# Pacing a background weight preparation by its own transfers, and a finer seam between two phases

## Chip, core and metric

One Trainium2 chip, one core of it, one launch. The metric is the time of an execution on the device in microseconds (us), as the median of several runs. Beside it stands one profiled execution, from which all rows below come; its span runs from the first instruction of the program to the last.

## What is computed

An attention over 4 batches and 8 heads of 64 (512 local tokens with a window of 32 to each side, 32 global tokens that see and are seen by all) and behind it two layers of a feed-forward kind, 512 to 2048 to 512, each without a residual. Weights of the second layer are `moe2`. Inputs are 32-bit floats but the weights arrive as 64-bit ones.

```
    a_l = sm(s_l)                        # local queries: 32 global keys and the window
    out_l = np.matmul(a_l, np.concatenate([v_g, v_l], axis=2))
    out_g = np.matmul(sm(s_g), v_all)    # global queries: all keys
...
    h = x @ w_in                         # first layer
    relu6 = np.clip(h + 3.0, 0.0, 6.0)
    g = h * relu6 / 6.0
    return (g @ w_out).astype(np.float32)
...
    h = x @ w_in                         # second layer
    alpha = 1.0
    g = np.where(h > 0.0, h, alpha * (np.exp(np.minimum(h, 0.0)) - 1.0))
    return (g @ w_out).astype(np.float32)
```

## The kernel before

The 2176 tokens are 17 tiles of 128 (16 local ones and `G`, the global tokens of all batches), put together to five chunks of 4, 3, 3, 3 and 4 tiles. Products keep about the accuracy of 32-bit floats by cutting each operand into a rounded part and a rest (`high`, `low`, names ending in h and l) and adding three matmuls (`mm3`, L541, where nearly all matmuls are recorded).

**Order of work.** The start is an order written out by hand (`SCHED`). From then on the program is a list of steps (layer, chunk, f), f being one of 16 blocks of 128 of the inner 2048. A step has `up` (12 matmuls into the tile h), `act` (on ScalarE g at L567 and the cast gh at L573, on VectorE the product at L568 and the rest gl), and `down` of the step two before it (`LAG`), which adds to the tiles acc. A step has three places (part 0, 1, 2), with the two halves of `down` between them. At these places stands other work: while chunk c runs, the attention of chunk c+1 in stages (scores S on TensorE at L349, minimum on VectorE, exponentials P on ScalarE at L362; transposes T at L90 and their copies PT; values O; then x), and at the end of a place the weight preparation. At the last block of a chunk the tiles acc are copied to `ev` (L603 on ScalarE, L605 on VectorE, three buffers) and stored to `x2d` (L607). Each engine, and SP, which issues all DMAs, works off its own instructions in the order in which the program writes them.

**The second layer.** Chunk 1 (`STD2`) is computed like the first layer, in 16 steps after the last of layer one. The chunks (2, 3) and (0, 4) are computed in pairs by class `Super`, with seven products (`up(g, k)` into ua and ub) in place of eight for each of 8 pairs of blocks and each pair of chunks. Product k of ua may be added to the tile ua only when ScalarE has copied what stands in it (tiles s, L790, L797, L800). `go` issues the next product or the next group of output matmuls (`down_a` into acc, `down_b` into yt) and then what `after(n, ...)` has put off by n turns.

**The preparation.** `prepare` is a generator that makes the second layer's weights ready while layer one runs, in eight pairs p of blocks: for each of four raw pieces of 512 KB a load (`load`, L163, tile raw), `first` (ScalarE, L167: scales the upper word into wi or wo), `second` and `third` (VectorE, L170 to L176: put the bits together), `high` (ScalarE cast, L182: tiles ha, hb, oa, ob), `low` (VectorE, L186) and `out` (L189: store of 512 KB to `wd`); in between the sums `sf` of the pieces for the seven products, cast and stored as sa and sb. Six stores for each pair. Later `load_stream` (L726) loads wd back as the tiles ws. Four buffers f0 to f3 take all of it, in the roles A, B_, W and X; what writes a buffer has to wait for the store or the readers of what it held.

The generator yields (gap, VectorE cost, ScalarE cost) ahead of each piece. `Pace.step` is called once at each place, three times a step; it lets a piece go when the last piece lies `gap` places back and when the work that it has counted for the two engines leaves room:

```
                gap, dve, act = self.cost
                if self.gap < gap or (dve and self.dve + dve > ROOM) or (act and self.act + act > ROOM):
                    return
```

Of the kernel before, what the change touches and what calls it, by code (L numbers as in the profile page):

```python
# [26 lines left out]
NF = DFF // P  # L27
# [32 lines left out]
ROOM = 2.25  # L60
# [8 lines left out]
def tile_kernel(ctx, tc, qkW, vW, qkG, vN, vG, masks, w1, w2, out):  # L69
# [83 lines left out]
    def prepare():  # L153
# [3 lines left out]
        def roles(p):  # L157
            return ("f0", "f2", "f1", "f3") if p % 2 == 0 else ("f2", "f0", "f3", "f1")

# [32 lines left out]
        nxt = load(0, 0, 0, "f0"), load(0, 1, 0, "f2")  # L192
        for p in range(NF // 2):
            A, B_, W, X = roles(p)
            ra, rb = nxt
            yield 1 if p else 3, 0, 1.2
# [3 lines left out]
            first(wb, rb)  # L200
            yield 1, 0.7, 0
            second(w)
            yield 0, 1.4, 0
            third(wa, ra)
            yield 0, 1.4, 0.6
            ha = high(shaped(wa, 2), 2, f"ha{p}", X)
            third(wb, rb)
            yield 0, 0.7, 0.6
            oa = load(p, 0, 1, B_)
            hb = high(shaped(wb, 2), 2, f"hb{p}", A)  # L210
            low(ha, shaped(wa, 2))
            yield 1, 0.7, 0
            low(hb, shaped(wb, 2))
            yield 1, 0, 0
            out(ha, p, 0)
            yield 1, 0, 0
            out(hb, p, 2)
            yield 2, 0.8, 0
# [3 lines left out]
            nc.vector.tensor_sub(sf[:, 0], sf[:, 2], half(wa, 0))  # L222
            yield 0, 0.8, 0
            nc.vector.tensor_sub(sf[:, 1], half(wa, 0), half(wb, 0))
            nc.vector.tensor_sub(sf[:, 3], half(wa, 1), sf[:, 0])
            yield 0, 0, 0.6
            s1 = high(sf[:, :2], 2, f"sa{p}", W)
            yield 1, 0.7, 0.6
            s2 = high(sf[:, 2:], 2, f"sb{p}", A)
            low(s1, sf[:, :2])  # L230
            yield 1, 0.7, 0
            low(s2, sf[:, 2:])
            yield 1, 0, 0
            out(s1, p, 8)
            yield 1, 0, 0.6
            out(s2, p, 10)
            w = pool.tile([P, 2, DM], I32, name=f"wo{p}", tag=X, bufs=1)
            wa, wb = w[:, 0], w[:, 1]
            first(wa, oa)
            yield 0, 0.4, 0  # L240
            second(wa)
            ob = load(p, 1, 1, W)
            yield 0, 1.4, 0
            third(wa, oa)
            yield 1, 0, 1.2
            ha = high(shaped(wa, 1), 1, f"oa{p}", A)
            first(wb, ob)
            yield 1, 1.1, 0
            low(ha, shaped(wa, 1))
            second(wb)  # L250
            yield 0, 1.4, 0
            if p + 1 < NF // 2:
                nxt = (load(p + 1, 0, 0, B_),)
            third(wb, ob)
            yield 1, 0, 0.6
            out(ha, p, 4)
            hb = high(shaped(wb, 1), 1, f"ob{p}", W)
            yield 1, 0.7, 0
            low(hb, shaped(wb, 1))
            if p + 1 < NF // 2:  # L260
                nxt += (load(p + 1, 1, 0, A),)
            yield 1, 0, 0
            out(hb, p, 6)

    class Pace:
# [788 lines left out]
```

## Time and profile before

| | |
|---|---|
| median of 3 runs | 880.34 us (878.87 to 880.65) |
| the profiled execution | 884.33 us, its span 882.3 us |
| TensorE (PE) busy | 851.4 us, 97% of the span |
| VectorE (DVE), ScalarE (ACT) busy | 516.7 us (59%), 429.1 us (49%) |
| granted clock of TensorE, mean | 0.992 |
| moved by DMA | 178.42 MB, 202 GB/s |

A busy share is a mean over stages: the start (to 85 us), layer one with the attention of the next chunk (to about 420), its last chunk without attention (to 513), the plain chunk of the second layer (to 585) and the paired chunks (to the end). Idle time stands in brackets behind an instruction in the timelines, with the instruction that ended it.

### The profile page before, as it was taken

What the parts mean: (1) busy time and instruction counts of PE and PEld (TensorE: products, weight loads), DVE (VectorE), ACT (ScalarE), POOL (GpSimd) and SP (SyncE); (2) the same over time, 40 slices, a digit from 0 to 9 for tenths busy, and PEclk for the clock granted to TensorE, in tenths of its full rate; (3) what the DMA queues carried; (4) which work ended last, traced back from release to release, by engine and by line L of the source; (5) the groups of instructions that cost most, each with busy time, mean ns of one, the idle gap of its engine ahead of it and who ended that gap; (6) DMA issues with size and microseconds to landing.
All of it is one profiled execution on the core that took longest, in us unless ns stands there. A gap on an engine that the chain in (4) does not pass through costs nothing.

```text
span 882.3 us, 15805 instructions
## 1 busy us (share of the span) xinstructions
PE 851.4 (97%) x6424; PEld 731.6 (83%) x6424; DVE 516.7 (59%) x1123; ACT 429.1 (49%) x835; POOL 4.8 (1%) x8
## 2 busy tenths in 40 slices
PE   8899999999799997999899999999999999999998
PEld 7667878898699886989788889988899888888886
DVE  5888974565547655666565544435456674444453
ACT  6576654454444434554443334545454664444442
POOL 0000000000000000000010000000000000000000
PEclk9999999999999999999999999999999999999999
DMA  9947223566645666663678973558662738444102
GB/s 370 418 190 318 81 96 107 176 198 221 220 166 199 225 226 200 216 218 106 217 258 294 352 272 157 204 188 312 238 247 88 286 133 321 143 143 143 48 1 95
DMA packets 37656, 178.42 MB, mean 202 GB/s; under 512 B 4304, under 2 KB 6224, under 8 KB 25680
## 3 DMA queue, kind: packets, MB, share of 16 engines
q1 hardware_dynamic: 37584, 177.42, 55.6%
q8 instruction: 50, 0.82, 0.4%
q14 instruction: 22, 0.18, 0.1%
HBM read 143.33 MB, written 34.08 MB: 201 GB/s over the span
## 4 chain that ended last, share of the span: by engine, by line
PE 75%; DVE 9%; DMA 9%; ACT 5%; issue 2%; SPq 0%; ACTq 0%; DVEq 0%
PE acc L541 26%; PE h L541 19%; PE yt L541 9%; PE ua L541 9%; PE ub L541 6%; DMA wd<-sa 2%; DMA raw<-in_w 2%; DMA wd<-ha 2%; PE T L90 2%; DMA v<-in_vW 1%; DVE g L568 1%; PE O L381 1%; DVE f L134 1%; PE S L349 1%; ACT g L567 1%
## 5 line engine op out<-in xcount | busy, mean ns | idle before, releaser
L541 PE MATMUL acc<-gh,w 128*128 128x384 f32 (+1 forms) x640 | 199.5, 366 | 3.4 <-DVE ev L605 1.7
L541 PE MATMUL h<-x1h,w 128*128 128x384 f32 (+1 forms) x640 | 198.1, 371 | 1.6 <-DVE w L148 1.5
L541 PEld LDWEIGHTS h<-x1h,w 128*128 128x128 f32 x640 | 120.6, 192 | 20.4 <-issue 5.5
L541 PEld LDWEIGHTS acc<-gh,w 128*128 128x128 f32 x640 | 118.7, 188 | 17.9 <-DVE ev L605 2.5
L541 PE MATMUL h<-x1l,w 128*128 128x384 f32 (+1 forms) x320 | 116.7, 365 | 0.2 <-DVE x1l L413 0.2
L541 PE MATMUL acc<-gl,w 128*128 128x384 f32 (+1 forms) x320 | 115.3, 360 | 0.8 <-DVE gl L575 0.8
L573 ACT CAST gh<-g 128x384 fp32r<-128x384 f32 (+1 forms) x96 | 52.8, 550 | 81.5 <-DVE g L568 71.5
L541 PE MATMUL ua<-xs,ws 128*128 128x384 f32 (+1 forms) x384 | 88.0, 364 | 2.1 <-ACT s L790 1.5
L568 DVE SCALAR_TENSOR_TENSOR g<-g,h 128x384 f32<-128x384 f32 (+1 forms) x80 | 48.4, 605 | 65.0 <-ACT g L567 64.6
L541 PEld LDWEIGHTS ua<-xs,ws 128*128 128x128 f32 x384 | 70.3, 188 | 12.9 <-ACT s L790 1.8
L575 DVE TENSOR_TENSOR gl<-g,gh 128x384 fp32r<-128x384 f32 (+1 forms) x96 | 57.4, 598 | 25.9 <-ACT gh L573 25.3
L567 ACT ACTIVATE g<-h,half 128x384 f32<-128x384 f32 (+1 forms) x80 | 49.7, 621 | 39.8 <-PE h L541 39.6
L541 PEld LDWEIGHTS h<-x1l,w 128*128 128x128 f32 x320 | 61.4, 192 | 6.1 <-DVE x1l L413 0.5
L541 PE MATMUL ub<-xs,ws 128*128 128x384 f32 (+1 forms) x288 | 65.7, 363 | 0.0
L541 PEld LDWEIGHTS acc<-gl,w 128*128 128x128 f32 x320 | 60.2, 188 | 6.4 <-DVE gl L575 1.2
L541 PEld LDWEIGHTS ub<-xs,ws 128*128 128x128 f32 x288 | 52.7, 188 | 7.1
L842 DVE TENSOR_TENSOR y<-yt,y 128x512 f32<-128x512 f32 x49 | 33.8, 690 | 34.6 <-PE yt L541 34.1
L757 ACT ACTIVATE e<-c 128x384 f32<-128x384 f32 (+1 forms) x48 | 27.8, 579 | 51.3 <-DVE c L793 19.6
L541 PE MATMUL yt<-ws,gg_h 128*128 128x512 f32 x160 | 49.9, 393 | 0.0
L541 PE MATMUL acc<-ws,gg_h 128*128 128x512 f32 x160 | 49.9, 393 | 0.0
L760 DVE SCALAR_TENSOR_TENSOR e<-e,c 128x384 f32<-128x384 f32 (+1 forms) x48 | 30.0, 624 | 26.0 <-ACT e L758 25.4
L758 ACT ACTIVATE e<-e 128x384 f32<-128x384 f32 (+1 forms) x64 | 37.1, 579 | 2.0
(201 smaller groups left out, 1269.2 us busy)
## 6 DMA issues: line engine op xcount, KB each, us to landing
ws<-wd SPq DMA_DIRECT2D x48, 1024.0 KB, 5.3
raw<-in_w SPq DMA_DIRECT2D x16, 1024.0 KB, 11.6
raw<-in_w SPq DMA_DIRECT2D x32, 512.0 KB, 4.6
v<-in_vW SPq DMA_DIRECT2D x13, 1040.0 KB, 7.1
qk<-in_qkW SPq DMA_DIRECT2D x15, 704.0 KB, 6.1
qkG<-in_qkG SPq DMA_DIRECT2D x8, 608.0 KB, 5.1
wd<-ha SPq DMA_DIRECT2D x8, 512.0 KB, 7.9
wd<-hb SPq DMA_DIRECT2D x8, 512.0 KB, 8.4
```

The source lines that it names most:

```text
L90: nc.tensor.transpose(o, i, ident)
L134: nc.vector.scalar_tensor_tensor(w, self.high[:, s], -0x80000000, w, op0=ALU.bitwise_and, op1=ALU.bitwise_or)
L349: nc.tensor.matmul(self.sp[r][cs, j, :], self.q[rs, j, cs], self.k[rs, j, 32 * i : 32 * i + P], start=True, stop=True,)
L541: nc.tensor.matmul(o, a, b, start=first and i == 0, stop=last and i == len(pairs) - 1, skip_group_check=more)
L567: nc.scalar.activation(g, hp, AF.Relu, scale=1.0 / 6.0, bias=half)
L568: nc.vector.scalar_tensor_tensor(g, g, 1.0, hp, op0=ALU.min, op1=ALU.mult)
L573: nc.scalar.copy(gh, g)
L575: return lambda: nc.vector.tensor_sub(gl, g, gh.bitcast(F32))
L757: nc.scalar.activation(e, h, AF.Relu, scale=-1.0)
L758: nc.scalar.activation(e, e, AF.Exp, scale=-1.0)
L760: 1, lambda: nc.vector.scalar_tensor_tensor(e, e, -1.0, h, op0=ALU.add, op1=ALU.max)
L842: nc.vector.tensor_add(y, o, y)
```

## The change

`FETCH` and `STORE` are two new constants, 3 each. `Pace` counts places in `now` from its start, and a piece names the place from which it may go: three places behind the load whose data it reads (`tw`, `ta`, `tb` hold that place), three behind the store of the buffer that it overwrites, one behind the cast whose rest it takes, two behind the computation whose result it stores. The roles of the four buffers are dealt out otherwise: ha and hb are cast into the buffers of their own raw pieces (A and B_), the sums stand in X, sa and sb follow ha and hb, and all raw pieces of `w_out` go through W. `first` and `second` of two pieces are apart. `step` also runs in the second layer while pieces are left, with costs for what stands there, and a pair of blocks is loaded back only when `done` says that its stores are issued. At the end of the plain chunk `go` is called behind every group of three output matmuls in place of every half of `down`, and the activation of c21 is put off by two turns in place of one.

```diff
-ROOM = 2.25
+ROOM, FETCH, STORE = 2.25, 3, 3
...
-        def roles(p):
-            return ("f0", "f2", "f1", "f3") if p % 2 == 0 else ("f2", "f0", "f3", "f1")
...
-        nxt = load(0, 0, 0, "f0"), load(0, 1, 0, "f2")
+        A, B_, W, X = "f0", "f2", "f1", "f3"
+        ra, rb = load(0, 0, 0, A), load(0, 1, 0, B_)
+        ta = tb = pace.now
         for p in range(NF // 2):
-            A, B_, W, X = roles(p)
-            ra, rb = nxt
-            yield 1 if p else 3, 0, 1.2
+            yield ta + FETCH, 0, 0.6
             w = pool.tile([P, 2, DM], I32, name=f"wi{p}", tag=W, bufs=1)
             wa, wb = w[:, 0], w[:, 1]
             first(wa, ra)
-            first(wb, rb)
-            yield 1, 0.7, 0
-            second(w)
+            yield pace.now + 1, 0.4, 0
+            second(wa)
             yield 0, 1.4, 0
             third(wa, ra)
-            yield 0, 1.4, 0.6
-            ha = high(shaped(wa, 2), 2, f"ha{p}", X)
+            yield tb + FETCH, 0, 0.6
+            first(wb, rb)
+            yield pace.now + 1, 0.4, 0.6
+            ha = high(shaped(wa, 2), 2, f"ha{p}", A)
+            second(wb)
+            yield 0, 1.4, 0
             third(wb, rb)
             yield 0, 0.7, 0.6
-            oa = load(p, 0, 1, B_)
-            hb = high(shaped(wb, 2), 2, f"hb{p}", A)
             low(ha, shaped(wa, 2))
-            yield 1, 0.7, 0
+            la = pace.now
+            hb = high(shaped(wb, 2), 2, f"hb{p}", B_)
+            yield pace.now + 1, 0.7, 0
             low(hb, shaped(wb, 2))
-            yield 1, 0, 0
-            out(ha, p, 0)
-            yield 1, 0, 0
-            out(hb, p, 2)
-            yield 2, 0.8, 0
+            lb = pace.now
+            yield 0, 0.8, 0
             sf = pool.tile([P, 4, 2 * P], F32, name=f"sf{p}", tag=X, bufs=1)
             half = lambda v, k: v.bitcast(F32)[:, 2 * P * k : 2 * P * k + 2 * P]
             nc.vector.tensor_add(sf[:, 2], half(wb, 0), half(wb, 1))
             nc.vector.tensor_sub(sf[:, 0], sf[:, 2], half(wa, 0))
+            yield la + 2, 0, 0
+            out(ha, p, 0)
+            ta = pace.now
             yield 0, 0.8, 0
             nc.vector.tensor_sub(sf[:, 1], half(wa, 0), half(wb, 0))
             nc.vector.tensor_sub(sf[:, 3], half(wa, 1), sf[:, 0])
-            yield 0, 0, 0.6
-            s1 = high(sf[:, :2], 2, f"sa{p}", W)
-            yield 1, 0.7, 0.6
-            s2 = high(sf[:, 2:], 2, f"sb{p}", A)
+            tw = pace.now
+            yield lb + 2, 0, 0
+            out(hb, p, 2)
+            tb = pace.now
+            yield tw + 2, 0, 0
+            oa = load(p, 0, 1, W)
+            tw = pace.now
+            yield ta + STORE, 0, 0.6
+            s1 = high(sf[:, :2], 2, f"sa{p}", A)
+            yield pace.now + 1, 0.7, 0
             low(s1, sf[:, :2])
-            yield 1, 0.7, 0
+            la = pace.now
+            yield tb + STORE, 0, 0.6
+            s2 = high(sf[:, 2:], 2, f"sb{p}", B_)
+            yield pace.now + 1, 0.7, 0
             low(s2, sf[:, 2:])
-            yield 1, 0, 0
+            lb = pace.now
+            yield la + 2, 0, 0
             out(s1, p, 8)
-            yield 1, 0, 0.6
-            out(s2, p, 10)
+            ta = pace.now
+            yield tw + FETCH, 0, 0.6
             w = pool.tile([P, 2, DM], I32, name=f"wo{p}", tag=X, bufs=1)
             wa, wb = w[:, 0], w[:, 1]
             first(wa, oa)
+            yield lb + 2, 0, 0
+            out(s2, p, 10)
+            tb = pace.now
             yield 0, 0.4, 0
             second(wa)
-            ob = load(p, 1, 1, W)
             yield 0, 1.4, 0
             third(wa, oa)
-            yield 1, 0, 1.2
+            yield pace.now + 2, 0, 0
+            ob = load(p, 1, 1, W)
+            tw = pace.now
+            yield ta + STORE, 0, 0.6
             ha = high(shaped(wa, 1), 1, f"oa{p}", A)
+            yield pace.now + 1, 0.7, 0
+            low(ha, shaped(wa, 1))
+            la = pace.now
+            yield tw + FETCH, 0, 0.6
             first(wb, ob)
-            yield 1, 1.1, 0
-            low(ha, shaped(wa, 1))
+            yield pace.now + 1, 0.4, 0
             second(wb)
+            yield la + 2, 0, 0
+            out(ha, p, 4)
+            ta = pace.now
             yield 0, 1.4, 0
+            third(wb, ob)
+            tw = pace.now
+            yield tb + STORE, 0, 0.6
+            hb = high(shaped(wb, 1), 1, f"ob{p}", B_)
+            yield pace.now + 1, 0.7, 0
+            low(hb, shaped(wb, 1))
+            lb = pace.now
+            yield tw + 2, 0, 0
             if p + 1 < NF // 2:
-                nxt = (load(p + 1, 0, 0, B_),)
-            third(wb, ob)
-            yield 1, 0, 0.6
-            out(ha, p, 4)
-            hb = high(shaped(wb, 1), 1, f"ob{p}", W)
-            yield 1, 0.7, 0
-            low(hb, shaped(wb, 1))
+                ra = load(p + 1, 0, 0, W)
+            tw = pace.now
+            yield lb + 2, 0, 0
+            out(hb, p, 6)
+            pace.done = p + 1
+            yield ta + STORE, 0, 0
             if p + 1 < NF // 2:
-                nxt += (load(p + 1, 1, 0, A),)
-            yield 1, 0, 0
-            out(hb, p, 6)
+                rb = load(p + 1, 1, 0, A)
+            ta, tb = tw, pace.now
+            A, B_, W, X = W, A, X, B_
 
...
-        def __init__(self, work, n):
-            self.work, self.left, self.gap = work, n, 0
-            self.cost = next(work)
+        def __init__(self):
+            self.now = self.done = 0
             self.dve = self.act = 0.0
+            self.cost = 0, 0, 0
+
+        def start(self, work):
+            self.work, self.cost = work, next(work)
         def step(self, long, dve, act):
+            self.now += 1
             self.dve = max(0.0, self.dve - long) + dve
             self.act = max(0.0, self.act - long) + act
-            self.gap += 1
             while self.cost is not None:
-                gap, dve, act = self.cost
-                if self.gap < gap or (dve and self.dve + dve > ROOM) or (act and self.act + act > ROOM):
+                earliest, dve, act = self.cost
+                if self.now < earliest or (dve and self.dve + dve > ROOM) or (act and self.act + act > ROOM):
                     return
                 self.dve, self.act = self.dve + dve, self.act + act
-                self.gap = 0
                 self.cost = next(self.work, None)
+
+    pace = Pace()
...
-    def down(m, c, f, part):
+    def down(m, c, f, part, then=None):
...
             mm3(acc[i], pairs, f == 0, f == NF - 1)
             if f == NF - 1:
                 drain(m, c, i)
+            if then is not None:
+                then()
...
                 nc.vector.tensor_add(c21, self.b, self.s2)
-                self.after(1, lambda: self.act(g, 2, c21))
+                self.after(2, lambda: self.act(g, 2, c21))
...
-        pace = Pace(prepare(), NF)
+        pace.start(prepare())
+        back = 0
...
-                if m == 0:
+                if m == 1:
+                    loads = [(1.2 * (part == 1 and 3 <= f < 12), 1.1 * (part == 1 and 5 <= f < 12)) for part in range(3)]
+                if pace.cost is not None:
...
                 if part == 0 and cur is not None:
                     late()
                 if part < 2:
-                    down(*old, part)
-                    if cur is None:
-                        sup.go()
-            if old[:2] == (0, last) and old[2] % 2:
-                sup.load_stream(-1 - old[2] // 2)
+                    down(*old, part, sup.go if cur is None else None)
+            while back < NF // 2 and old >= (0, last, 2 * back + 1) and pace.done > back:
```

What this does to the order is shown at three places. First ScalarE where chunk 2 of layer one begins (g_2_0 is its first activation, P the exponentials of its first attention tile, wo, oa and raw_1_... belong to pair 1). Before:

```order
L573 CAST gh_1_15_2764<-g_1_15_2763 128x384
L167 ACTIVATE wo_2770<-raw_1_0_1_2568 128x512
L182 CAST oa_2784<-wo_2770 128x512
L167 ACTIVATE wo_2770<-raw_1_1_1_2773 128x512
L567 ACTIVATE g_2_0_2808<-h_2_0_2795,half 128x384
L573 CAST gh_2_0_2809<-g_2_0_2808 128x384
L362 ACTIVATE P_2814<-P_2814,mn_2818 128x128 x8
```

Of the change:

```order
L605 CAST gh_1_15_2765<-g_1_15_2764 128x384
L164 ACTIVATE wo_2771<-raw_1_0_1_2703 128x512
L599 ACTIVATE g_2_0_2803<-h_2_0_2790,half 128x384
L605 CAST gh_2_0_2804<-g_2_0_2803 128x384
L394 ACTIVATE P_2809<-P_2809,mn_2813 128x128 x8
L179 CAST oa_2873<-wo_2771 128x512
```

The cast oa and the `first` of the second output piece (raw_1_1_1) stood ahead of g_2_0, gh_2_0 and P; now oa stands behind P, and that `first` is no longer among these rows.

Second, SP and ScalarE where chunk 3 begins, with pair 3. SP before (v and qk are loads of the attention, the stores to wd and raw of the preparation):

```order
L320 DMA qk_3795<-in_qkW 128x1408
L189 DMA wd_76<-ha_3708 128x1024
L189 DMA wd_76<-hb_3733 128x1024
L328 DMA v_0_3903<-in_vW 128x2080
L189 DMA wd_76<-sa_3847 128x1024
L189 DMA wd_76<-sb_3868 128x1024
L163 DMA raw_3_1_1_3936<-in_w 128x1024
L320 DMA qk_4030<-in_qkW 128x1408
```

SP of the change:

```order
L352 DMA qk_3782<-in_qkW 128x1408
L360 DMA v_0_3892<-in_vW 128x2080
L186 DMA wd_76<-ha_3816 128x1024
L186 DMA wd_76<-hb_3858 128x1024
L160 DMA raw_3_0_1_3940<-in_w 128x1024
L352 DMA qk_4016<-in_qkW 128x1408
L186 DMA wd_76<-sa_3942 128x1024
```

ScalarE of the change at the same place:

```order
L599 ACTIVATE g_2_15_3918<-h_2_15_3905,half 128x384
L605 CAST gh_2_15_3919<-g_2_15_3918 128x384
L179 CAST sa_3942<-sf_3901 128x2x256
L599 ACTIVATE g_3_0_3957<-h_3_0_3944,half 128x384
L605 CAST gh_3_0_3958<-g_3_0_3957 128x384
L394 ACTIVATE P_3963<-P_3963,mn_3967 128x128 x8
```

The stores of ha and hb stood ahead of the load of v and now stand behind it, with the first output piece; the load of the second (raw_3_1_1) has left these rows. The cast sa, into the buffer of ha, is the last thing on ScalarE ahead of the chunk's first activation.

Third, TensorE at the seam from the plain chunk (acc) to the paired ones (ua and ub, xs being their operands). Before:

```order
L541 MATMUL acc_1_2_5875<-ws-8_1_5850,gl_1_14_6263 128x512
L541 MATMUL ub_2_6334<-xs_2_6010,ws_0_6209 128x384 x6
L541 MATMUL acc_1_0_5873<-ws-8_1_5850,gh_1_15_6298 128x512 x2
L541 MATMUL acc_1_0_5873<-ws-8_1_5850,gl_1_15_6299 128x512
L541 MATMUL acc_1_1_5874<-ws-8_1_5850,gh_1_15_6298 128x512 x2
L541 MATMUL acc_1_1_5874<-ws-8_1_5850,gl_1_15_6299 128x512
L541 MATMUL ua_6322<-xs_6_6043,ws_2_6213 128x384 x6
L541 MATMUL acc_1_2_5875<-ws-8_1_5850,gh_1_15_6298 128x512 x2
L541 MATMUL acc_1_2_5875<-ws-8_1_5850,gl_1_15_6299 128x512
L541 MATMUL ub_7_6373<-xs_7_6076,ws_2_6213 128x384 x6
L541 MATMUL ua_6322<-xs_5_6109,ws_2_6213 128x384 x6
L541 MATMUL ua_6322<-xs_3_6142,ws_2_6213 128x384 x6
```

Of the change:

```order
L573 MATMUL acc_1_2_5857<-ws-8_1_6022,gh_1_14_6270 128x512 x2
L573 MATMUL acc_1_2_5857<-ws-8_1_6022,gl_1_14_6271 128x512
L573 MATMUL ua_6327<-xs_6_6051,ws_2_6221 128x384 x6
L573 MATMUL acc_1_0_5855<-ws-8_1_6022,gh_1_15_6306 128x512 x2
L573 MATMUL acc_1_0_5855<-ws-8_1_6022,gl_1_15_6307 128x512
L573 MATMUL ub_7_6369<-xs_7_6084,ws_2_6221 128x384 x6
L573 MATMUL acc_1_1_5856<-ws-8_1_6022,gh_1_15_6306 128x512 x2
L573 MATMUL acc_1_1_5856<-ws-8_1_6022,gl_1_15_6307 128x512
L573 MATMUL ua_6327<-xs_5_6117,ws_2_6221 128x384 x6
L573 MATMUL acc_1_2_5857<-ws-8_1_6022,gh_1_15_6306 128x512 x2
L573 MATMUL acc_1_2_5857<-ws-8_1_6022,gl_1_15_6307 128x512
L573 MATMUL ua_6327<-xs_3_6150,ws_2_6221 128x384 x6
```

The rows with xs_6, xs_7, xs_5 and xs_3 now have a group of acc between every two of them; xs_5 and xs_3, both into ua, stood back to back.

## Rows read from the trace of the kernel before

**Rows 1.** Page, part 1: busy us (share) and instructions of each engine.

```profile
PE 851.4 (97%) x6424; PEld 731.6 (83%) x6424; DVE 516.7 (59%) x1123; ACT 429.1 (49%) x835; POOL 4.8 (1%) x8
```

**Rows 2.** Windows: stretch, us, busy of each engine (x instructions), PEclk, DMA share, GB/s.

```profile
205.00:258.00 53.00, 48.06 (x511) 43.68 (x510) 28.30 (x78) 22.33 (x48) 0.00 (x0) 0.94 0.61 212
240.00:244.00 4.00, 4.00 (x15) 3.56 (x15) 1.60 (x3) 2.10 (x6) 0.00 (x0) 0.50 0.03 12
442.00:585.00 143.00, 143.00 (x668) 122.41 (x667) 71.47 (x113) 58.76 (x104) 4.05 (x2) 1.00 0.69 249
600.00:868.00 268.00, 268.00 (x1234) 228.05 (x1233) 145.69 (x228) 129.01 (x231) 0.00 (x0) 1.00 0.45 166
```

**Rows 3.** Waits, whole span: who waited for whom, us in total, times, longest.

```profile
ACT oa L182 <- DMA wd<-sb: 16.9, 8, 6.4
...
PE T L90 <- ACT P L362: 9.8, 2, 5.0
```

**Rows 4.** Timeline of ScalarE: start, us, line, op, idle before and releaser.

```profile
233.15 0.62 ACT L182 CAST oa<-wo 128x512 fp32r<-128x512 f32 x1 [2.77 <-DMA wd<-sb]
236.43 0.66 ACT L167 ACTIVATE wo<-raw 128x512 f32<-128x512 f32 x1 [2.67 <-DMA raw<-in_w]
...
238.60 2.45 ACT L362 ACTIVATE P<-P,mn 128x128 f32<-128x128 f32 x8
```

**Rows 5.** Timeline of TensorE at the two stalls, same columns.

```profile
239.14 2.44 PE L90 MATMUL T<-ident,P 128*128 128x128 f32 x8 [4.82 <-ACT P L362]
...
337.58 2.44 PE L90 MATMUL T<-ident,P 128*128 128x128 f32 x8 [5.03 <-ACT P L362]
```

**Rows 6.** Chain that ended last, in order of time: start us, us, what.

```profile
231.85 4.56 DMA raw<-in_w
...
241.57 3.84 PE h L541 x12
...
259.46 1.49 PE T L90 x8
...
340.02 2.56 PE h L541 x12
...
540.07 2.08 PE h L541 x12
542.15 2.06 PE acc L541 x9
...
573.24 2.08 PE h L541 x12
```

**Rows 7.** Timeline of SP (DMA issue): start, us.

```profile
321.74 0.33 SPq L328 DMA_DIRECT2D v<-in_vW  x1
```

**Rows 8.** Source line 189 (stores of the preparation): time to landing.

```profile
DMA to landing us min/median/max: 2.6/6.0/10.5
```

**Rows 9.** DMA issues: count, KB each, median us to landing.

```profile
wd<-ha SPq DMA_DIRECT2D x8, 512.0 KB, 7.9
...
wd<-sa SPq DMA_DIRECT2D x8, 512.0 KB, 4.2
...
ws-8_1_5850<-wd SPq DMA_DIRECT2D x1, 1024.0 KB, 11.1
```

**Rows 10.** Timeline of ScalarE at the border to chunk 4.

```profile
428.76 0.67 ACT L167 ACTIVATE wo<-raw 128x512 f32<-128x512 f32 x1 [1.91 <-DMA raw<-in_w]
...
436.16 0.85 ACT L603 COPY ev<-acc 128x384 f32<-128x384 f32 x2
```

**Rows 11.** Timeline of TensorE: border to chunk 4 and seam, idle in brackets.

```profile
436.69 0.50 PE L541 MATMUL acc<-gh,w 128*128 128x512 f32 x1 [1.68 <-ACT ev L603]
...
439.92 0.50 PE L541 MATMUL acc<-gh,w 128*128 128x512 f32 x1 [0.88 <-DVE ev L605]
...
591.52 1.31 PE L541 MATMUL ua<-xs,ws 128*128 128x384 f32 x6 [0.57 <-ACT s L800]
...
597.49 1.32 PE L541 MATMUL ua<-xs,ws 128*128 128x384 f32 x6 [1.52 <-ACT s L790]
```

More of the change, by code (lines that the diff above doesn't have):

```diff
@@ L965, in tile_kernel @@
                 if part < 2:
-                    down(*old, part)
-                    if cur is None:
-                        sup.go()
-            if old[:2] == (0, last) and old[2] % 2:
-                sup.load_stream(-1 - old[2] // 2)
+                    down(*old, part, sup.go if cur is None else None)
+            while back < NF // 2 and old >= (0, last, 2 * back + 1) and pace.done > back:
+                sup.load_stream(-1 - back)
+                back += 1
         while sup.groups:
```

## Prediction

> **What bounds the kernel now.** The page comes first: TensorE is busy 851.4 us of a span of 882.3 [rows 1]. So a change that takes no matmul away can win at most the 30.9 us in which it is not, and the time that a lowered clock costs. The windows by stage say where that is. In 442 to 585 and in 600 to 868 TensorE is busy in every microsecond [rows 2]: nothing is to be won there, only lost. In 205 to 258 it is idle for 4.9 us. The list of waits names the cause: the transposes T of the attention waited for the exponentials on ScalarE twice, 9.8 us in all, 5.0 the longer, and nothing else on TensorE waited as long [rows 3]. The timeline of ScalarE shows what stood ahead of the exponentials: the cast oa sat 2.77 us for a store of sb, then the next conversion 2.67 us for its raw weights, and only then came the work of the chunk and the exponentials at 238.60 [rows 4]. The second stall, at 337.58, is the same sequence one chunk later [rows 5]. ScalarE works in the order written, so a wait for a transfer there holds everything that is written behind it.
>
> After the stall TensorE is also slower. The granted clock of 240 to 244 is 0.50 [rows 2], the lower level (1.2 GHz), after 4.8 us of idling. In the chain T took 2.44 us at both stalls [rows 5] and 1.49 without one, twelve matmuls of h took 3.84 and 2.56 behind the two stalls, and 2.08 at the full clock [rows 6].
>
> **The change, part by part.** *Waits of ScalarE ahead of the attention.* The first place shown from the order says it: where the cast oa and the second conversion stood ahead of g, gh and the exponentials of chunk 2, both now stand behind them. The raw weights were asked for at 231.85 and landed 4.56 us later [rows 6]; ScalarE was there at 233.8. Now a conversion stands at least three places behind its load, and three places are one step of the loop. What goes: the two stalls, 9.8 us, and the slow clock behind them, 2 x (2.44 - 1.49) + (3.84 - 2.08) + (2.56 - 2.08) = 1.9 + 1.8 + 0.5 = 4.1 us. Together 13.9.
>
> Something is late next at the second of the two. There, before the chunk's first scores, the order puts the cast sa, which writes the buffer that ha is being stored from; the store of ha is issued right behind the load of v, which went out at 321.74 [rows 7]. A store has landed 2.6 to 10.5 us after its issue [rows 8], in the median 7.9 for ha, which travels with other transfers, and 4.2 for sa [rows 9]. From a ScalarE instruction that ends a wait to the exponentials it took 238.60 - 236.43 = 2.2 us [rows 4]. If ha lands 7.9 us after about 322.1, sa starts at 330.0, the exponentials at 332.2 and end 2.45 us later at 334.7. TensorE is ready for T at 337.58 - 5.03 = 332.55 and would end it 1.49 later at 334.0, so 0.7 is lost. With 10.5 us it is 3.3, with 4.2 nothing. I take 1.3, since this store has a 1 MB load directly ahead of it. So 13.9 - 1.3 = **12.6**.
>
> The Trainium skill (DMA: Bandwidth & Descriptors, section "Anatomy of one DMA — SWDGE (gpsimd) path") counts some 2 us fixed and the bytes at 436 GB/s for one transfer; as an estimate from that page a 512 KB store takes 3.2 us, the leftover of 1.3 would be none and the sum 1.3 larger. The rows disagree where a store has company (7.9 above).
>
> *The border of chunks 3 and 4.* ScalarE reached the copy ev only at 436.16, behind a conversion that had waited 1.91 us for raw weights and the cast ob [rows 10]; TensorE waited 1.68 us for that copy and 0.88 for a later one, on VectorE, whose buffer was still being stored [rows 11]. In the new order only g, gh and a cast whose input is old stand ahead of ev. Both waits go: **2.6**. The bound from below is 1.7, if the second stays.
>
> *The seam to the grouped products.* TensorE idled 0.57 and 1.52 us because ua may be added to only when ScalarE has copied it [rows 11]. The third place from the order shows a group of acc matmuls now between every two products, and the two ua products that stood back to back apart; the activation of c21 moves one turn later, so that the copy of the next group's ua no longer stands behind it. I leave 0.2 at each: **1.7**. From both sides: 0 if another ScalarE instruction fills the place, 2.1 if both go. In 600 to 868, where the later c21 holds for every group, TensorE is never idle and ScalarE is busy 129 of 268 us [rows 2]; its consumer is the last of the group's, so I cost the delay at nothing.
>
> *What is added.* The shift on VectorE is cut in two for each pair, eight more instructions, at most as long as the cast of 0.62 [rows 4], so under 5 us on an engine that is busy 28 of 53 us [rows 2]: nothing. The last pair ends in the second layer, where ScalarE is busy 59 and VectorE 71 of 143 us [rows 2]. A step there is 2.08 + 2.06 = 4.1 us and h has two banks, so ScalarE may be most of a step late before TensorE notices: nothing. On SP's queue every load and store of the preparation keeps its place between the attention's loads or moves by one or two; SP is in order too, and a load that waits for a store to land (the second raw load of a pair) holds the attention's next load. Before, eight casts oa waited 16.9 us for stores [rows 3], and only at the two stalls did TensorE notice. New waits of that kind will come where three places are shorter than a store in company. Between nothing and one stall of 5.0 I take **0.7** as loss, nearer to nothing because at the other scores twice as much matmul work lies between S and T as at the two stalls.
>
> **The sum:** 12.6 + 2.6 + 1.7 - 0.7 = 16.2 us. The profiled execution took 884.33 (882.3 and 2.0 around it); it would take 868.1. The median of the runs, 880.34, is 4.0 lower; 880.34 - 16.2 = **864.1**.
>
> **The rivals.** (a) *A store wait takes the place of the raw wait.* A cast behind a store of 8 to 10 us stands ahead of some exponentials or PT copies, and one stall of 5.0 with up to 2 of slow clock comes back: 869 to 871. For it: three places are 4 to 6 us, the median store of ha 7.9. Against: SP mostly issues ahead of TensorE. Chance 0.12. (b) *Stores are home in time*, all like the 4.2 of sa: no leftover, 880.34 - 17.5 = 862.8. For it: SP, with fewer waits ahead, may issue earlier. Against: the load of v in front. Chance 0.10. (The rule of the Trainium skill named above would have it so.) (c) *More goes than I count*, small waits of the attention that I left alone: 858 to 860. Chance 0.05. (d) *Nothing changes:* the loads are late because SP's queue is, wherever the conversion stands. But at 231.85 the load was issued only 1.9 us ahead of the place where ScalarE wanted it; that is order, not the queue. Chance 0.03. (e) *Slower: the last pair is late for its own layer.* Its last store now stands in step 6 of the second layer, and its reload waits for that to land. That step starts at 540.07 and ends near 544.2; the longest store is 10.5 [rows 8] and the reload ws-8_1 took 11.1 [rows 9], so the weights are there by 565.8, and TensorE wants them at 573.24 [rows 6]: 7.4 us to spare. Beyond them each microsecond late costs one; to end slower than before by more than 0.2% it takes 7.4 + 16.2 + 1.8, some 25 us. Against it: the places are counted, so a late transfer does not push the later places away. Chance 0.04.
>
> **How the numbers follow.** The forecast, 0.66, has its own range of 861 to 867: leftovers from 0 to 3.3, the seam from 0 to 2.1, new waits from 0 to some 2. The range given reaches to (a) above and near (c) below: 859.5 to 871. About 0.2% (1.8 us; the three runs lie 878.87 to 880.65) is what a measurement of this kernel can tell from no change. Faster: 0.66 + 0.12 + 0.10 + 0.05 = 0.93; same 0.03; slower 0.04.
>
> **What would show it.** T <- ACT P at most some 2 us in the list of waits, and at chunk 3's first T alone; the granted clock at 1.00 in the stretches of the two stalls; no idle of TensorE for ev at the border to chunk 4; under 0.5 us at the seam; ScalarE's waits for raw weights small, those of sa, sb and oa for stores what remains; the second layer still without a gap, with ws-8 landed several microseconds before its first matmul. The prediction is wrong if T still waits for P for more than 4 us in all, if a cast that waits for a store stands ahead of a TensorE wait somewhere new, or if TensorE is idle between 442 and 585.

## The result and the profile after

The changed kernel took **867.86 us** in the median of 4 runs (866.25 to 868.54); the kernel before, beside it, 879.80. The ratio is 0.9862 (0.9844 to 0.9880): 11.9 us less, where 16.2 were forecast (864.1 us). The time lies in the range given and 3.8 us above the forecast.

The profiled execution took 867.5 us with a span of 865.6. The first part of its page, against [rows 1]:

```profile
PE 845.4 (98%) x6424; PEld 729.1 (84%) x6424; DVE 517.5 (60%) x1131; ACT 429.7 (50%) x835; POOL 4.6 (1%) x8
```

TensorE does the same 6424 matmuls in 6.0 us less busy time, and it idles 20.2 us in place of 30.9. Less of the busy time is at the lower clock (mean granted clock 0.996 for 0.992), and less of it is in rows of T that wait for P inside (see the stalls below).

The list of waits of the changed kernel (who waited for whom: us in all, times, longest), against [rows 3]:

```profile
ACT ob L179 <- DVE wo L173: 10.8, 8, 2.4
...
PE S L381 <- DVE x1l L445: 5.4, 5, 2.4
ACT oa L179 <- DMA wd<-sa: 4.6, 1, 4.6
...
ACT sa L179 <- DMA wd<-ha: 3.9, 1, 3.9
...
PE T L90 <- ACT P L394: 0.7, 1, 0.7
```

The transposes T wait 0.7 us for P where they waited 9.8. In their place stands a wait that the prediction did not have: the scores S wait 5.4 us for x1l. TensorE's timeline shows where, with the idle time ahead in brackets:

```profile
248.87 1.95 PE L381 MATMUL S<-qk 64*32 64x128 f32 x62 [2.40 <-DVE x1l L445]
...
327.69 2.29 PE L90 MATMUL T<-ident,P 128*128 128x128 f32 x8 [0.75 <-ACT P L394]
...
341.64 1.14 PE L381 MATMUL S<-qk 64*32 64x128 f32 x62 [1.15 <-DVE x1l L445]
```

The windows of the changed kernel (columns as in [rows 2]) show the clock behind the first of these (second row), and that the stretch from ahead of the border to chunk 4 to behind the seam (400 to 590) and the paired chunks have no gap:

```profile
400.00:590.00 190.00, 190.00 (x910) 165.00 (x909) 109.00 (x184) 89.63 (x167) 3.85 (x2) 1.00 0.71 257
248.00:252.00 4.00, 3.13 (x66) 2.75 (x67) 2.85 (x14) 0.85 (x4) 0.00 (x0) 0.57 0.84 314
585.00:852.00 267.00, 267.00 (x1229) 227.14 (x1228) 144.06 (x226) 129.18 (x229) 0.00 (x0) 1.00 0.46 171
```

**What made x1l late.** VectorE's timeline of the changed kernel at the border to chunk 2:

```profile
243.46 0.56 DVE L639 COPY ev<-acc 128x384 f32<-128x384 f32 x1 [1.00 <-DMA x2d<-ev]
243.93 0.68 DVE L170 SCALAR_TENSOR_TENSOR wo<-raw,wo 128x512 int32<-128x512 int32 x1
244.65 0.69 DVE L173 SCALAR_TENSOR_TENSOR wo<-raw,wo 128x512 int32<-128x512 int32 x1
246.51 0.55 DVE L600 SCALAR_TENSOR_TENSOR g<-g,h 128x384 f32<-128x384 f32 x1 [1.17 <-ACT g L599]
248.12 0.69 DVE L445 TENSOR_TENSOR x1l<-XT,x1h 128x512 fp32r<-128x512 f32 x1 [1.06 <-ACT x1h L444]
```

And ScalarE's, same kernel and place:

```profile
245.37 0.62 ACT L179 CAST ob<-wo 128x512 fp32r<-128x512 f32 x1 [1.97 <-DVE wo L173]
245.90 0.57 ACT L599 ACTIVATE g<-h,half 128x384 f32<-128x384 f32 x1
247.09 0.51 ACT L605 CAST gh<-g 128x384 fp32r<-128x384 f32 x1 [0.62 <-DVE g L600]
247.51 0.58 ACT L444 CAST x1h<-XT 128x512 fp32r<-128x512 f32 x1
```

The copy ev waits for an older ev to be stored. Behind it stands `third`, 1.4 us of bit work. The cast ob, let go at the same place as the `third` whose result it reads, holds ScalarE until that is done, and g, gh and x1h of the chunk stand behind ob. S and the transposed x take turns in the same two banks (`att`), so S waits until x1l has been read from there. No transfer of the preparation takes part: it is a piece that stands too close behind another piece.

### The profile page after: what moved, and what is told of

Read it like the earlier page. It is cut to its first block, busy times and chain, and to the rows that moved or that the text cites. A ratio compares the mean times of both kernels' runs of the same rounds, so it can differ in the third digit from the quotient of the medians.

```text
span 865.6 us, 15837 instructions
## 1 busy us (share of the span) xinstructions
PE 845.4 (98%) x6424; PEld 729.1 (84%) x6424; DVE 517.5 (60%) x1131; ACT 429.7 (50%) x835; POOL 4.6 (1%) x8
## 4 chain that ended last, share of the span: by engine, by line
PE 84%; DVE 7%; DMA 4%; ACT 3%; issue 1%; SPq 0%; ACTq 0%; DVEq 0%
PE acc L573 30%; PE h L573 23%; PE ua L573 9%; PE yt L573 9%; PE ub L573 7%; DMA v<-in_vW 2%; PE S L381 1%; PE T L90 1%; PE O L413 1%; DVE f L134 1%; DVE g L600 1%; DVE f L137 1%; PE SG L503 1%; DMA wd<-ha 1%; DMA x2d<-ev 1%
## 5 line engine op out<-in xcount | busy, mean ns | idle before, releaser
L573 PE MATMUL h<-x1h,w 128*128 128x384 f32 (+1 forms) x640 | 196.0, 367 | 1.7 <-DVE w L148 1.5
L573 PEld LDWEIGHTS h<-x1h,w 128*128 128x128 f32 x640 | 118.7, 189 | 20.7 <-issue 5.7
```

The lines of the kernel that those rows point to most:

```text
L573: nc.tensor.matmul(o, a, b, start=first and i == 0, stop=last and i == len(pairs) - 1, skip_group_check=more)
```

## Experiments

Times are medians of a kernel's runs, ratios are to the kernel before on the same chip. Its median was 880.18 us beside e1 to e4, 882.33 beside e5 to e8 and 880.61 beside e9 to e11.

**The kernel before, again** (e1, and later e9 and e10, a single execution each; no edit).

> The kernel before, unchanged, run again to see where its profiled execution (884.33 us) spent the 4.0 us that it lies above the median of its runs. Theory A: in the two stalls of T and the slow clock behind them, which differ from execution to execution; then a second profile at 879 to 881 us shows T waiting 5 to 8 us in all instead of 9.8, a mean granted clock of 0.994 to 0.996 instead of 0.992, and the runs' times follow their clocks. Theory B: elsewhere (the start, or a general slowness); then the second profile has T <- ACT P near 9.8 again and the difference lies ahead of 88 us or spread over all stages. Ratio to itself 0.999 to 1.001.

> The kernel before once more, for the stalls of another execution. So far three profiled executions with its preparation had T <- ACT P at 9.8 us (884.33), 8.0 (888.11) and 4.3 (876.08, with the new seam). Theory A: the two stalls differ by several us from execution to execution with the landing of raw weights, and the time follows: T <- ACT P between 4 and 10 us in all, and each us of it goes with 1.0 to 1.5 us of time. Theory B: the time of an execution does not follow its T stalls.

> As the run before it: the kernel before, another execution. Theory A: T <- ACT P between 4 and 10 us in all, the time 877 to 884 in step with it. Theory B: no such relation.

Measured: e1 881.93 us (879.03 to 888.11, 12 runs), ratio to itself 1.0013 (0.9992 to 1.0033); e9 882.20; e10 879.56. The wait of T in the lists of the three profiles, e1 (888.11 us) first, then e9, then e10:

```profile
PE T L90 <- ACT P L362: 8.0, 3, 4.5
```

```profile
PE T L90 <- ACT P L362: 4.4, 2, 2.4
```

```profile
PE T L90 <- ACT P L362: 3.9, 2, 2.2
```

With the first profile (9.8) and e2's below (4.3) that makes five executions of one preparation with 3.9 to 9.8 us. The execution on which the sum was made is the one with the longest stalls, and its 884.33 us were 4.0 above the median. The time follows the stalls only in part. e1's profile has 1.8 us less of this wait than the first and took 3.8 us longer; among what it lost elsewhere, TG waited 2.7 us for PG in place of 0.9. And e9 is 2.6 us longer than e10 with nearly the same T; on TensorE's line 1.7 us of that lie ahead of 62 us, in the start of the program. So of Theory A the spread of the stalls holds; that each us of T goes with 1.0 to 1.5 us of time does not come out of these executions.

Where the difference at the first stall comes from shows on SP. In the first profile of the kernel before, then in e10 (start, us of issue):

```profile
226.70 0.32 SPq L189 DMA_DIRECT2D wd<-sa  x1
```

```profile
226.17 0.32 SPq L189 DMA_DIRECT2D wd<-sa  x1
228.30 0.32 SPq L189 DMA_DIRECT2D wd<-sb  x1
229.29 0.33 SPq L163 DMA_DIRECT2D raw<-in_w  x1
```

The load raw goes into the buffer that sa is stored from, and waits for that store: 3.1 us behind its issue in e10, 5.15 us in the first profile, where it went out at 231.85 [rows 6]. With stores that landed later T idled 4.82 us here in the first profile [rows 5], with these 1.67. The other executions agree here: 5.17 us and a T of 4.53 in e1, 3.36 and 1.93 in e9. At the second stall the landing of sa alone does not order them (in e2 it took 5.0 us there, and T waited 2.11). Why the same store lands sooner in one execution than in another, no run shows.

**The seam alone on the kernel before** (e2).

```diff
-                    down(*old, part)
-                    if cur is None:
-                        sup.go()
+                    down(*old, part, sup.go if cur is None else None)
...
-                self.after(1, lambda: self.act(g, 2, c21))
+                self.after(2, lambda: self.act(g, 2, c21))
```

> The kernel before with the seam part alone (go behind every group of three output matmuls, c21 two turns later); the preparation is as before. Theory: the two waits for s at the seam (0.57 and 1.52 us) go and nothing takes their place, so 1.7 to 2.3 us less, 877.5 to 878.1 us, ratio 0.9975, and the two T stalls stand as before. Rival: the plain chunk ends earlier but another ScalarE instruction fills the place, or the later c21 costs as much in the 16 groups; then 879.8 us, ratio 1.000, with the idle time at another product of ua or ub.

Measured: 878.41 us (875.46 to 880.62), ratio 0.9969 (0.9951 to 0.9987). No ua waits for s any more, and the stalls of T stand (2.15 and 2.11 in its profile). The interval, 1.1 to 4.3 us, holds the 1.7 to 2.3 of the theory and leaves out the rival's nothing.

**One conversion later on the kernel before** (e3).

```diff
-            yield 1, 0, 1.2
+            yield 1, 0, 0.6
             ha = high(shaped(wa, 1), 1, f"oa{p}", A)
+            yield 3 if p in (1, 3) else 0, 0, 0.6
             first(wb, ob)
```

(`step` also runs in the second layer, so that the last pieces are let go.)

> The kernel before, in which the conversion of the second output piece alone stands three places later for pairs 1 and 3, behind the exponentials at the two stalls; the cast oa, which waits for the store of sb, stays ahead of them. Theory: the wait for the raw weights (2.67 us) and the conversion itself (0.66) are what made T late; T then waits 4.8 - 3.3 = 1.5 us at each, and most of the slow clock behind it goes: 2 x 3.3 and 2 to 4 us of clock, 9 to 10 less than a profiled execution like the first, 6 to 9 less in the median, 871 to 874 us. Rival 1: the store wait ahead of the cast is enough by itself: T still waits 4 us or more and the time is 878 to 880. Rival 2: the conversion moved behind the exponentials holds the copies PT and O or x1 wait in place of T: 876 to 880, with an idle place a few us later.

Measured: **888.38 us**, ratio 1.0089 (1.0063 to 1.0116), slower, beyond what any theory had; Rival 2 comes nearest. At the first stall T waited even less than the 1.5 us expected, but it waits again at the next tile:

```profile
235.85 2.29 PE L90 MATMUL T<-ident,P 128*128 128x128 f32 x8 [0.86 <-ACT P L363]
...
260.89 2.52 PE L90 MATMUL T<-ident,P 128*128 128x128 f32 x8 [4.62 <-ACT P L363]
```

What held that one, on ScalarE and SP of the same kernel:

```profile
259.89 0.66 ACT L167 ACTIVATE wi<-raw 128x512 f32<-128x512 f32 x1 [9.33 <-DMA raw<-in_w]
```

```profile
246.21 0.44 SPq L189 DMA_DIRECT2D wd<-oa  x1
...
255.10 0.33 SPq L163 DMA_DIRECT2D raw<-in_w  x1
```

The conversion moved by three places moved the store of oa with it: in the first profile it was issued ahead of the border, at 234.67, here behind the load of v of the border. The next pair's load goes into the buffer of oa and went out only 8.9 us behind that store. The next pair's conversion did not move: on ScalarE it stands right behind x1h in both (first piece at 253.07 in the first profile, at 249.89 here), and P of the next tile waits behind its second piece, at both borders (T 4.62 and 3.06 us).

Of the old stall this shows the part of the raw wait and the conversion: T waits 0.86 and 0.60 us, against 1.67 to 2.45 in e9 and e10, whose cast oa waits for bit work, as here, and not for a store. What a store wait ahead of the cast adds (2.77 us in the first profile, Rival 1) this execution cannot tell, as it had none. To move one wait without the ones behind it makes a longer one.

**The border held** (e4, on the changed kernel; inside `if m == 0`).

```diff
+                    if f == 1:
+                        loads[2][0] += 1.0
```

> The changed kernel, with one more microsecond of VectorE work counted at the last place of step 1 of each chunk (where the copies ev stand), so that no piece with bit work is let go there. By the order, third and the cast ob then stand behind x1h and x1l of chunk 3's first tile, and at the next border the cast sa stands behind the exponentials and their copies. Theory: the two new waits of the scores for x1l (2.40 and 1.15 us, the first with slow clock behind it, 3.0 and 1.0 together) come from third on VectorE and the cast behind it on ScalarE, and the leftover at T (0.75 and 0.8 of a slower T) from sa: 5.5 less than the changed kernel, 862.4 us, range 860.5 to 864. Rival 1: it is the copies ev, which wait 1.0 and 2.0 for the stores to x2d, that hold x1l; then both waits of S stay and only the leftover goes: 866. Rival 2: the pieces held back wait or hold something at a later place: 867 to 868.

Measured: **862.32 us** (861.20 to 864.76), ratio 0.9790 (0.9763 to 0.9818). The theory's number. S does not wait at the first of the two places, and 0.28 us at the second. VectorE's timeline at the first of them has `third` behind x1l now:

```profile
241.80 0.56 DVE L639 COPY ev<-acc 128x384 f32<-128x384 f32 x1 [1.15 <-PE h L573]
...
244.05 0.69 DVE L445 TENSOR_TENSOR x1l<-XT,x1h 128x512 fp32r<-128x512 f32 x1 [1.06 <-ACT x1h L444]
245.12 0.69 DVE L170 SCALAR_TENSOR_TENSOR wo<-raw,wo 128x512 int32<-128x512 int32 x1
```

ScalarE's copy ev still waits 2.05 us for its store there, as in the changed kernel, and S is on time: Rival 1 falls. One idle place above 0.3 us is left past 310 us, in the second layer, and behind it is the same pair, ob and `third`. TensorE's row, then ScalarE's:

```profile
532.97 0.45 PE L573 MATMUL h<-x2h,ws-5_0_5557 128*128 128x384 f32 x1 [1.05 <-DVE g L604]
```

```profile
530.76 0.62 ACT L179 CAST ob<-wo 128x512 fp32r<-128x512 f32 x1 [2.81 <-DVE wo L173]
```

**Short distances** (e5, on the changed kernel).

```diff
-ROOM, FETCH, STORE = 2.25, 3, 3
+ROOM, FETCH, STORE = 2.25, 1, 1
```

> The changed kernel with FETCH and STORE 1 in place of 3: a conversion may go one place behind its load and a cast one place behind the store of its buffer; roles, split pieces and the seam as in the changed kernel. Theory: the distance counted from the transfer is what took the waits off ScalarE. A place is 1.4 to 2 us and raw weights land in 5.4 us in the median, so ScalarE waits some 3 us at many of the 32 raw pieces (40 us or more in all, 12.7 with 3 places), T waits for P again for more than 5 us in all, some with slow clock behind it: 875 to 890 us. Rival: the new roles and the split pieces are enough, the counted distance adds little: 866 to 870.

Measured: 880.33 us (875.10 to 883.87), ratio 0.9970 (0.9949 to 0.9991). Its list of waits:

```profile
ACT wi L164 <- DMA raw<-in_w: 25.4, 12, 4.5
...
ACT wo L164 <- DMA raw<-in_w: 10.5, 6, 3.2
```

By the ratios, 0.9970 against 0.9862, the distance is worth 9.5 us, most of what the change won, and the rival falls. The seam alone (e2) had 0.9969, so the new roles and the split pieces without the distance won nothing that these runs can tell; they mostly trade waits. FETCH and STORE were not tried apart, nor the distance with the old roles. The place was not as expected: T waits 0.4 us, and what ScalarE lost came out at S, at the scores SG and at one OG (2.38 us) of the global tiles.

**A longer distance** (e6, on the changed kernel): FETCH 4.

> The changed kernel with FETCH 4: each conversion one place later. By the order the last pair then ends in step 13 of the second layer in place of step 6, 7 x 4.14 = 29 us later on TensorE's line, where ws-8 landed 15.5 us before its first matmul. Theory (the mechanism of the slower rival): TensorE idles 29 - 15.5 = some 11 to 14 us for ws-8, 2 us of slow clock behind it, and what FETCH 4 saves or costs in layer one is within 3 us: 877 to 884 us, with one gap h <- DMA ws-8 in the second layer. Rival: SP and ScalarE run so far ahead of TensorE there that the reload is earlier than its step: under 4 us idle, 866 to 871.

Measured: 882.26 us (878.69 to 885.30), ratio 1.0002 (0.9984 to 1.0020). TensorE's one long gap:

```profile
571.92 0.66 PE L573 MATMUL h<-x2h,ws-8_0_6252 128*128 128x384 f32 x1 [9.61 <-DMA ws-8_0_6252<-wd]
```

The slower rival's mechanism is real, and one place more for each of four conversions of a pair is enough for it. The gap is a little under the 11 to 14 expected.

**The seam and the cast ob on the held kernel** (e7: the seam's two edits undone; e8: below; e11: e8 with c21 one turn later again).

```diff
-            yield tb + STORE, 0, 0.6
+            yield max(tb + STORE, pace.now + 1), 0, 0.6
             hb = high(shaped(wb, 1), 1, f"ob{p}", B_)
```

> The kernel with the border held (862.3 us), with the old seam put back: go behind every half of the output matmuls, c21 one turn later. Theory: the waits for s of 0.57 and 1.52 us come back at the same two products and nothing else changes: 2.1 to 2.4 us more, 864.4 to 864.7. Rival: without the earlier stalls something else hides them, 862.3, or the earlier c21 gives back time in the 16 groups, under 862.

> The kernel with the border held, and the cast ob one place behind the bit work whose result it reads (it could go at the same place). Theory: ScalarE then no longer stands at ob for VectorE (16.3 us in eight waits), g of the second layer is on time, and the one idle place of TensorE past 310 us (1.05 us ahead of ws-5) goes: 861.2 us, range 860 to 862. Rival: every later piece moves by up to one place for each pair, and one of them meets a score or a transpose: 862 to 866, with a new idle place that names it.

> The kernel with the border held and ob later (860.3 us), with c21's activation put back to one turn later; go stays behind every group of three. By the order the copy s_1 of the second group then stands behind the two activations of c21 again. Theory: the second wait of the seam (1.52 us, for that copy) comes back and the first (0.57) does not: 1.5 more, 861.8 us, one idle place of TensorE near 576 us. Rival: with groups of acc between the products the copy is early enough even so: 860.3, no idle place.

Measured: e7 866.65 us (863.44 to 867.78), ratio 0.9816, against 0.9790 for e4: 2.3 us by the ratios, in the range of the theory, though the runs of e7 spread over 4 us. e8 **860.32 us** (859.47 to 861.08), ratio 0.9749 (0.9724 to 0.9775), the fastest. e11 862.59 us, ratio 0.9787 (0.9761 to 0.9813). TensorE at the seam in e7, then in e11:

```profile
570.95 1.31 PE L573 MATMUL ua<-xs,ws 128*128 128x384 f32 x6 [0.57 <-ACT s L834]
...
576.91 1.31 PE L573 MATMUL ua<-xs,ws 128*128 128x384 f32 x6 [1.52 <-ACT s L824]
```

```profile
574.70 1.31 PE L573 MATMUL ua<-xs,ws 128*128 128x384 f32 x6 [1.52 <-ACT s L824]
```

So the finer `go` takes away the 0.57 and the later c21 the 1.52. The rows carry this more than the times do: the intervals of e7 and e4, and of e11 and e8, overlap, and e11 lost 2.3 us in the median for the 1.5 expected. In e8 ScalarE waits 4.9 us for wo at ob in place of 16.3, TensorE has no gap of 0.1 us past 351 us, and the stretch that held the first stall runs full:

```profile
205.00:258.00 53.00, 52.88 (x615) 48.59 (x614) 32.91 (x102) 26.58 (x60) 0.00 (x0) 1.00 0.71 231
```

## Why the prediction was right, and where its sizes were not

To see where the 11.9 us came from I set the starts of the same TensorE groups in e10 (879.56 us, near the median of the kernel before) beside those of the changed kernel's profile (867.5). Their ends on TensorE's line differ by 11.9 as well. It is one execution against one, and another pair would split the difference otherwise. Each row is what the difference grew by:

| stretch (e10 -> after, us) | grew by | forecast |
|---|---|---|
| start and border to chunk 1, to h 214.27 -> 215.00 | +0.7 | 0 |
| first T stall and its clock, to acc 241.22 -> 237.93 | -4.0 | -7.5 |
| new wait of S and its clock, to acc 253.14 -> 253.48 | +3.6 | new waits +0.7 |
| small waits of T and TG, to h 298.49 -> 295.95 | -2.9 | 0 |
| second T stall and its clock, to acc 336.96 -> 331.95 | -2.5 | -5.1 |
| new wait of S, to h 346.66 -> 342.71 | +1.1 | see above |
| small waits of T and TG, to h 393.41 -> 387.31 | -2.2 | 0 |
| border of chunks 3 and 4, to h 435.99 -> 426.30 | -3.6 | -2.6 |
| seam and the rest, to the end 873.68 -> 861.77 | -2.2 | -1.7 |

**The stalls** (13.9 less a leftover of 1.3). The mechanism was right, and so was the size against the execution that it was read from: set beside the first profile in the same way, after saves 7.9 and 4.9 there, 12.8 in all, where 12.6 were forecast. The step that failed is the last one of the sum, to take what one execution lost off the median of the others. In e10 the stalls with their clock were worth 6.5: T idled 1.67 and 2.21 us there, and the store of sa landed 2.0 and 1.5 us sooner than in the first profile. The leftover was as thought: at 325.01 ScalarE ended a wait of 3.88 us for the store of ha, T then idled 0.75 us and took 2.29 in place of 1.49.

One row was read wrongly, with little effect on the sum: the 2.44 us of T at the stalls were put down to the slow clock. In the changed kernel the T that took 2.29 us ran with the granted clock at 1.00:

```profile
327.60:329.60 2.00, 1.91 (x7) 0.97 (x7) 1.86 (x10) 2.00 (x8) 0.00 (x0) 1.00 0.40 149
```

The eight exponentials that it transposes one by one take 2.45 us [rows 4]; where P was early, T took 1.03 to 1.25 us in the changed kernel. So most of the 1.9 us (0.8 of the 0.95 at each stall) is ScalarE's pace, and goes when P is early.

**The new waits** (0.7). The wrong step is that this term counted only casts and loads that wait for a store, and that VectorE's bit work beside it was put at "nothing" on an engine that is busy 28 of 53 us. The mean hides the border, where VectorE first waits for a store and then has bit work ahead of x1l; the wait fell on S, not on T, where I had looked, and cost 4.7 in all. That third and ob together were its cause is shown by e4, which moved both; what each of the two took alone was not tried there (e8 moves ob alone, and what went with it is a wait in the second layer).

**What was not counted.** Many small waits of T and TG, together 5.1. In the two stretches TensorE idles 2.6 us in e10, at most 1.23 at once, and 0.4 in the changed kernel; much of the rest is in rows that take longer at the same clock, T first (1.97 and 1.74 us for 1.03). Rival (c), which had the small waits that I left alone go too, named them and had 0.05; they went, and the new waits took their place. So the forecast's error of 4 us is three errors: stalls 6.1 too large, new waits 4.0 too small, and other gains of some 6 left out.

**Border and seam** came out at 3.6 and 2.2 for 2.6 and 1.7, both a little more; at the border e10 waits 1.83 and 1.24 us for the 1.68 and 0.88 of the sum. e2, e7 and e11 show the seam's two halves; c21 later costs nothing in the other groups, as forecast (TensorE is never idle in 585 to 852).

**The rivals.** (a) A store wait in the raw wait's place came in small, at chunk 3 alone; the longest one left, 4.6 us of oa for the store of sa, is in the second layer, where TensorE does not idle. (b) Stores home in time: the transfers of the changed kernel, KB and median us to landing, against [rows 9]:

```profile
wd<-ha SPq DMA_DIRECT2D x8, 512.0 KB, 3.6
...
ws-8_0_6020<-wd SPq DMA_DIRECT2D x1, 1024.0 KB, 7.0
ws-8_1_6022<-wd SPq DMA_DIRECT2D x1, 1024.0 KB, 6.8
```

The median store of ha fell from 7.9 to 3.6, while those of sa and sb rose from 4.2 and 4.3 to 4.6 and 5.9. The Trainium skill (DMA: Bandwidth & Descriptors, "Anatomy of one DMA — SWDGE (gpsimd) path"), from which 3.2 was an estimate, is near the median of ha now, though its formula is for DMAs issued on the GpSimd path and these are issued by SP. At the place that counted, issued at 316.54 behind the load of v, the store still took 8.4, and there the row decides. (d) fell. (e) did not happen: the last reload, issued at 536.12, landed at 542.9, and TensorE came to these weights at 558.9, 16 us to spare for the 7.4 forecast; e6 spent them.

## What to carry to other kernels

Read the stall that you price in more than one execution: where an engine that works in order waits for transfers, its loss changes from one to the next (here 3.9 to 9.8 us), and the sum goes off the median of that loss, not off the one that was profiled. Distance between a transfer and its reader has to be given to all readers in a chain at once (e3 lost 8 us by giving it to one), and distance is paid at the chain's end (e6). When the transfers are off the path, the next thing to look for is a piece let go at the same place as the piece that feeds it from another engine: two small edits (e4, e8) took 7.5 us more (867.86 to 860.32; by the ratios, 9.9).

## What the runs showed of the hardware

The kernel with fewer waits spread less: the kernel before ran from 876.74 to 884.44 us in 23 runs on one chip, e8 from 859.47 to 861.08 in 5 on another. That the waits are the reason is not shown; e7, with the two short waits of the seam, spread over 4.3 us in 4 runs.

The clock does not follow from the idle time ahead alone. At the border to chunk 1 TensorE idled in two steps, in the changed kernel 0.64 and 1.43 us, in e10 1.18 and 1.10. TensorE's rows and the window of the changed kernel, then those of e10:

```profile
154.23 0.44 PE L573 MATMUL acc<-gh,w 128*128 128x384 f32 x1 [0.64 <-DVE ev L639]
156.78 1.96 PE L381 MATMUL S<-qk 64*32 64x128 f32 x62 [1.43 <-DVE x1l L445]
```

```profile
155.00:162.00 7.00, 5.57 (x81) 4.92 (x81) 4.23 (x20) 3.85 (x11) 0.00 (x0) 0.76 0.52 193
```

```profile
154.56 0.44 PE L541 MATMUL acc<-gh,w 128*128 128x384 f32 x1 [1.18 <-DVE ev L605]
156.78 1.14 PE L349 MATMUL S<-qk 64*32 64x128 f32 x62 [1.10 <-DVE x1l L413]
```

```profile
155.00:162.00 7.00, 5.90 (x91) 5.19 (x90) 4.43 (x21) 3.92 (x11) 0.00 (x0) 1.00 0.46 165
```

With 2.07 us of idling the mean granted clock of the 7 us was 0.76, so part of them ran at the lower level (1.2 GHz); with 2.28 it stayed at the upper one (2.4 GHz). The kernel before alone shows both: in its first profile 0.85 and 1.09 us at this border were followed by 0.76 over 154 to 161. So what a short stall costs in clock is not fixed, a second reason not to price it from one execution.
